# A convolution and two feed-forward layers on one core: chunk groups across the batch border, a later load of the second block, and part of the weight clipping on GpSimd

## The chip, the cores and the metric

The kernel runs on one core of a Trainium2 chip. A core has TensorE (PE: matrix products, and PEld, its loading of weights), VectorE (DVE), ScalarE (ACT), GpSimd (POOL) and SyncE (SP, which here issues nearly all transfers). Each engine works through its own instruction stream in order and waits for the others by semaphores. The metric is the device time of one execution in microseconds (us), the median of several runs.

## What is computed

There are two batches of 4096 tokens with 192 channels, so 8192 tokens. First a causal convolution over seven tokens with softmaxed taps per head, then two layers of width 2048 with weights given in float64:

```python
# convolution: 8 heads of 24 channels, 7 taps
w = softmax(weight)                       # (8, 7)
out[b, s] = sum_k w[h, k] * x_pad[b, s + k]
# layer 1
h = x @ w_in;  g = maximum(0.01 * h, h);  x = g @ w_out
# layer 2
h = x @ w_in
P = a0 + a1*h + a2*h**2 + a3*h**3
Q = 1 + |b0|*|h| + |b1|*h**2
out = (P / (Q + 1e-6)) @ w_out
```

Results are float32. Every matrix product is made of float32r products: each operand is split into a high part and a rest (`xh`/`xl`, `wiH`/`wiL`, `gH`/`gL`), and the products of the parts are added up in PSUM.

## The kernel before

The tokens are cut into 16 blocks of 512, the width of 2048 into 16 pieces j of 128. One piece of one layer for one block is five matmuls of 128x512 into a PSUM bank (`gemm1`), the nonlinearity on ACT, DVE and POOL, and five matmuls of 128x512 into an accumulator (`gemm2_hi` three, `gemm2_lo` two). Two layers, 16 blocks and 16 pieces of ten matmuls make 5,120 matmuls of 128x512.

The order is made at build time. `Planner.run` knows for each operation a rank, its engines with a cost in us, the operations before it and the buffers that it takes from a pool (four PSUM banks, 13 `work` tiles, 10 `pair` tiles, 3 `raw` tiles). It always places the operation that can start first by these costs, and where an operation names two engines (as `l2_Q`: ACT or POOL) it also picks the engine. The constants at the head of the file (`LEAD`, `STEP`, `OFF`, ...) are parts of the ranks. What the planner puts out is written down as each engine's stream, and the chip follows that order whatever the true durations are.

What matters around the change:

- **Start.** `s_warm` keeps PE at work on constants until the first data are there. The taps go to DRAM and come back as banded matrices (`s_get`, tile `band`). Blocks 0 and 1 are convolved directly: `load_x` into `xt`, `conv` (4 small products per half), `conv_evac`, transposes (`trans`), and the split into `xh`/`xl` (`x_hi`, `x_lo`). `s_fill` puts extra products on PE while it waits.
- **Blocks 2 to 15.** Chunks of 122 tokens are convolved in groups of up to five: `load_g`, `conv_g` for each half of the heads, `evac_g`, `put_g` to DRAM. `get_y`, `turn_y`, `y_hi`, `y_lo` bring them back as a block's input. `groups` is made for each batch on its own.
- **Weights.** 28 pieces, 14 a layer (`r`, `m`, `o`), come as 64-bit words and are made into float32 on the chip. In `convert`, ACT takes the magnitude (`cv_abs`) and the low word (`cv_low`), DVE clips and shifts (`cv_clip`: two instructions, lines 396 and 397, on a PSUM bank), and DVE puts the bits together (`cv_bits`: two instructions of line 250). Then ACT writes the high part (`w_hi`, `r_hi`) and DVE or POOL the rest (`w_lo`, `r_lo`).
- **End.** Layer 1 runs ahead of layer 2 by a block and more. After the last block's layer 1, its layer 2 (`l2_...`) stands alone.

Helpers record many operations, so a line of the profile is often a helper's: L253 is every matmul, L244 every activation, L247 tensor-tensor, L250 scalar-tensor-tensor, L670 `l2_Q` on POOL.

Of the kernel before, what the change touches and what calls it, by code (L numbers as in the profile page):

```python
# [27 lines left out]
STEP = 4.016
PULL = 0.005
WINDOW = 193.974  # L30
LOOK = 58
REST = -0.364
OFF = {'xfin_add': 27.93, 'xfin_main': -41.19, 'l2_rs': -6.51, 'l2_Q': -76.54, 'l2_lo': 20.05, 'cv_clip': 21.93, 'r_lo': -1.28, 'gemm2_lo': -4.32, 'fin_trans': 100.9, 'cv_abs': -25.96, 'gemm2_hi': -3.11, 'l2_R': -14.71, 'cv_low': -5.24, 'fin_evac': -75.01, 'trans': -38.96, 'mid_swap': -4.79, 'x_hi': 22.32, 'conv': -29.75, 'l2_p3': 3.44, 'r_hi': 17.48, 'x_lo': 2.67, 'fin_rest': -19.55, 'l2_abs': 22.74, 'l2_r': 2.84, 'l1_lo': -25.06, 'l2_D': -10.01, 'cv_bits': -8.15, 'l2_hi': -1.95, 'mid_add': -112.83, 'gemm1': -4.61, 'w_lo': -48.12, 'fin_add': -69.89, 'load_g': 63.41, 'conv_g': -23.42, 'evac_g': -35.87, 'put_g': 12.36, 'get_y': -27.55, 'turn_y': 19.29, 'y_hi': -15.46, 'y_lo': -20.59}
TAIL = 5.502
# [139 lines left out]
def conv_leaky_rational_kernel(  # L174
# [610 lines left out]
    on(DVE(0.4), -83, 0, s_seed, r=["qc"], w=[("xh", 1, 0, 0)])  # L785
    on(PE(0.6 * WARM + 2.2), -74, 0, s_warm, r=["ident", "qc", ("xh", 1, 0, 0)], w=[("acc", 0, 1)])
# [239 lines left out]
```

## Time and profile before

| | before |
|---|---|
| median of 3 runs | 1245.04 us (1243.78 to 1246.08) |
| the profiled execution's own time | 1244.22 us |
| its span, first to last instruction | 1242.4 us |
| busy share of PE, ACT, DVE, POOL | 98%, 92%, 90%, 85% |
| mean granted clock of TensorE | 0.996 |

The span is what the trace covers; 1.8 us of the execution's own time lie outside it. The profiled execution is 0.8 us below the median of the runs. Shares are of the span, and an average over stages of different kinds.

### The profile page before, as it was taken

To read this page: it belongs to the slowest core of one execution; us is meant where nothing else is said; L and a number is where in the kernel's file an instruction comes from. 1 tells how busy PE (TensorE), PEld (TensorE's weight loads), DVE (VectorE), ACT (ScalarE), POOL (GpSimd) and SP (SyncE) were. 2 spreads that over 40 slices of the span, in tenths; PEclk is the share of its full clock that TensorE was granted. 3 is DMA by queue.
4 is the path that set the end of the run, shared out by engine and by line. 5 is a ranking of instruction groups with operands and counts; after the bars stand their busy time and mean duration, and the time that the engine had idled before them with its cause. 6 is when DMAs were issued, how large, how long until landed. Compare 5 with 4: busy or idle time off the path is not lost.

```text
span 1242.4 us, 17891 instructions
## 1 busy us (share of the span) xinstructions
PE 1217.3 (98%) x5437; PEld 997.6 (80%) x5437; DVE 1112.0 (90%) x1671; ACT 1138.5 (92%) x1996; POOL 1059.2 (85%) x1000
## 2 busy tenths in 40 slices
PE   8999999999999999999999999999999999999976
PEld 7787788888888888888888888888888888888744
DVE  7999989898998989898988999898998989889898
ACT  6889999899999999999999999999999999999996
POOL 2787988989889898898888989899898888988886
PEclk9999999999999999999999999999999999999998
DMA  7752002020110201111010111010210002000000
GB/s 210 200 164 71 1 3 52 2 42 1 38 18 1 56 1 44 18 30 33 7 45 12 29 33 29 20 23 5 50 26 1 13 1 41 1 1 14 1 13 13
DMA packets 137414, 42.34 MB, mean 34 GB/s; under 512 B 113571, under 2 KB 134758, under 8 KB 137318
## 3 DMA queue, kind: packets, MB, share of 16 engines
q1 hardware_dynamic: 135702, 41.00, 14.3%
q8 instruction: 42, 0.69, 0.2%
q14 instruction: 54, 0.44, 0.1%
q10 hardware_dynamic: 1616, 0.21, 0.1%
HBM read 27.28 MB, written 11.80 MB: 31 GB/s over the span
## 4 chain that ended last, share of the span: by engine, by line
PE 81%; ACT 7%; DVE 7%; issue 2%; DMA 1%; POOL 1%; SPq 0%; POOLq 0%; DVEq 0%; ACTq 0%
PE bank L253 41%; PE acc L253 39%; ACT work L244 4%; DVE work L250 2%; ACT raw L244 1%; DMA raw<-in_moe_w_in_dram 1%; DVE bank L250 1%; DVE pair L247 1%; ACT bank L244 1%; DVE bank L396 1%; DVE bank L397 1%; DVE pair L250 1%; DVE work L247 0%; DVE raw L250 0%; POOL pair L247 0%
## 5 line engine op out<-in xcount | busy, mean ns | idle before, releaser
L253 PE MATMUL acc<-pair,wo 128*128 128x512 f32 x2560 | 657.4, 391 | 6.2 <-POOL pair L247 2.7
L253 PEld LDWEIGHTS acc<-pair,wo 128*128 128x128 f32 x2560 | 478.5, 188 | 110.6 <-POOL pair L247 6.9
L244 ACT ACTIVATE work<-work 128x512 f32<-128x512 f32 x532 | 331.4, 630 | 17.6 <-DVE work L250 11.0
L247 POOL TENSOR_TENSOR work<-work,pair 128x512 f32<-128x512 f32 x184 | 239.5, 1302 | 43.6 <-DVE pair L250 34.6
L253 PE MATMUL bank<-xh,wiH 128*128 128x512 f32 x512 | 203.5, 397 | 9.2 <-DVE raw L250 4.2
L253 PE MATMUL bank<-xh,wiL 128*128 128x512 f32 x512 | 200.2, 391 | 0.0
L253 PE MATMUL bank<-xl,wiH 128*128 128x512 f32 x512 | 200.0, 391 | 0.0
L253 PE MATMUL bank<-xl,wiR 128*128 128x512 f32 x512 | 200.0, 391 | 0.0
L253 PE MATMUL bank<-xh,wiR 128*128 128x512 f32 x512 | 199.9, 390 | 0.0
L250 DVE SCALAR_TENSOR_TENSOR work<-work,b_sb,bank 128x512 f32<-128x512 f32 x182 | 135.1, 742 | 46.5 <-ACT work L244 45.3
L247 POOL TENSOR_TENSOR pair<-work,work 128x512 fp32r<-128x512 f32 x122 | 158.0, 1297 | 20.4 <-DVE work L250 14.8
L250 DVE SCALAR_TENSOR_TENSOR work<-bank,a_sb,work 128x512 f32<-128x512 f32 x184 | 136.9, 744 | 9.6 <-POOL work L247 7.6
L244 ACT ACTIVATE work<-bank,a_sb 128x512 f32<-128x512 f32 x176 | 135.3, 769 | 6.1 <-PE bank L253 6.0
L250 DVE SCALAR_TENSOR_TENSOR pair<-bank,a_sb,work 128x512 fp32r<-128x512 f32 x168 | 125.2, 745 | 13.1 <-ACT work L244 7.8
L250 DVE SCALAR_TENSOR_TENSOR bank<-work,a_sb,bank 128x512 f32<-128x512 f32 x176 | 132.1, 752 | 4.1
L244 ACT ACTIVATE raw<-raw 128x512 f32<-128x512 f32 x202 | 126.8, 630 | 6.2 <-DVE raw L250 3.6
L253 PEld LDWEIGHTS bank<-xh,wiH 128*128 128x128 f32 x512 | 96.4, 188 | 38.1 <-DVE raw L250 6.6
L247 POOL TENSOR_TENSOR pair<-work,pair 128x512 fp32r<-128x512 f32 x92 | 120.3, 1308 | 7.0 <-PE acc L253 1.8
L244 ACT ACTIVATE work<-bank,b_sb 128x512 f32<-128x512 f32 x182 | 124.0, 681 | 0.0
L247 DVE TENSOR_TENSOR work<-work,bank 128x512 f32<-128x512 f32 x176 | 119.3, 678 | 1.3 <-ACT raw L244 1.3
L253 PEld LDWEIGHTS bank<-xl,wiH 128*128 128x128 f32 x512 | 96.5, 189 | 20.7 <-DVE xl L247 0.3
L253 PEld LDWEIGHTS bank<-xl,wiR 128*128 128x128 f32 x512 | 96.4, 188 | 20.6 <-DVE xl L247 0.3
(104 smaller groups left out, 1954.5 us busy)
## 6 DMA issues: line engine op xcount, KB each, us to landing
work<-y_dram SPq DMA_DIRECT2D x108, 64.0 KB
raw<-in_moe_w_out_dram SPq DMA_DIRECT2D x16, 384.0 KB
...
```

Of the source, the lines that this page charges most:

```text
L244: nc.scalar.activation(out=out_, in_=in_, func=func, **k)
L247: (eng or nc.vector).tensor_tensor(out=out_, in0=in0, in1=in1, op=op)
L250: nc.vector.scalar_tensor_tensor(out=out_, in0=in0, scalar=s, in1=in1, op0=op0, op1=op1)
L253: nc.tensor.matmul(out=out_, lhsT=w, rhs=r, start=start, stop=stop)
L396: nc.vector.tensor_scalar(out=a, in0=a, scalar1=F64_TINY, scalar2=F64_HUGE, op0=ALU.max, op1=ALU.min)
L397: nc.vector.tensor_scalar(out=ai, in0=ai, scalar1=3, scalar2=0x3FFFFFF8, op0=ALU.logical_shift_left, op1=ALU.bitwise_and)
```

## The change

Four things are done, and the ranks are set anew with them.

1. `chunks` runs through both batches, and `groups` cuts it in fives. There were 13 groups (for one batch 5, 5, 4, 4, 4, 4 chunks, for the other six of 5 and one of 4); now there are 12 of 5. The number of chunks (60) stays.
2. `load_x` of block 1 waits for both halves of `band`; `load_g` may start at rank 30 and not 8.
3. `cv_clip` is parted. The clip is an operation of its own that works in place on a `work` tile in SBUF and may go to DVE or POOL; `cv_shift` reads it and writes the PSUM bank `cb`, which `cv_bits` then uses. So a bank is held from the shift on, and no longer from `cv_abs` on.
4. `s_warm` is 13 products of 128x256, and the 19 products on a seeded tile (`s_seed`, `SHAPES`) are gone. `SP`'s cost in the planner takes 300 and not 350 KB per us.

In the new order 14 of the 28 clips are on POOL. `l2_Q` is on POOL 196 times and not 178, `l1_hi` 110 and not 93; `y_lo` is there 20 times and not 25, `w_lo` 15 and not 18, `r_lo` 3 and not 6.

```diff
-LEAD = 66.057
-GAP = 6.373
-PREP = 56.276
+LEAD = 57.54
+GAP = 12.887
+PREP = 19.279
...
-OFF = {'xfin_add': 27.93, 'xfin_main': -41.19, 'l2_rs': -6.51, ...
+OFF = {'xfin_add': 41.11, 'xfin_main': -97.37, 'l2_rs': -47.59, ...
...
-        return [("SP", max(0.6 * count, nbytes / 350e3))]
+        return [("SP", max(0.6 * count, nbytes / 300e3))]
...
-    groups = []
+    chunks = []
     for bi in range(B):
-        t0 = max(blocks[DIRECT][3] - bi * S, 0) if bi == 0 else 0
-        count = -(-(S - t0) // CG)
-        starts = [min(t0 + c * CG, S - CG) for c in range(count)]
-        ng = -(-count // NTC)
-        at = 0
-        for g in range(ng):
-            k = min(NTC, -(-(count - at) // (ng - g)))
-            groups.append((bi, starts[at:at + k], t0 + at * CG))
-            at += k
+        t0 = blocks[DIRECT][3] if bi == 0 else 0
+        while t0 < S:
+            s0 = min(t0, S - CG)
+            chunks.append((bi, s0, t0 - s0))
+            t0 = s0 + CG
+    groups = [chunks[c:c + NTC] for c in range(0, len(chunks), NTC)]
...
     def s_warm(eng):
         for n in range(WARM):
             mm(acc[0][1][:, 0:WIDE], ident, qc[:, 0:WIDE], True, True)
-        t = xh[1][0][0]
-        for cols, count, step in SHAPES:
-            for n in range(count):
-                k = n * step % 4
-                mm(acc[0][1][:, 0:cols], t[:, k * P:(k + 1) * P], t[:, 0:cols], True, True)
...
     def cv_clip(eng, l, kind, q, n):
         a = buf[("cq", l, kind, q)][:, 0:n]
-        ai = a.bitcast(I32)
-        nc.vector.tensor_scalar(out=a, in0=a, scalar1=F64_TINY, scalar2=F64_HUGE, op0=ALU.max, op1=ALU.min)
-        nc.vector.tensor_scalar(out=ai, in0=ai, scalar1=3, scalar2=0x3FFFFFF8,
+        (nc.gpsimd if eng == "POOL" else nc.vector).tensor_scalar(out=a, in0=a, scalar1=F64_TINY, scalar2=F64_HUGE,
+                                                                  op0=ALU.max, op1=ALU.min)
+
+    def cv_shift(eng, l, kind, q, n):
+        nc.vector.tensor_scalar(out=buf[("cb", l, kind, q)].bitcast(I32)[:, 0:n],
+                                in0=buf[("cq", l, kind, q)].bitcast(I32)[:, 0:n], scalar1=3, scalar2=0x3FFFFFF8,
                                 op0=ALU.logical_shift_left, op1=ALU.bitwise_and)
...
-        on(ACT(t_act(w, True)), c, 0, cv_abs, *a, w, r=[raw] + spare, w=[cq], take=("spare" if early else "bank", cq))
+        on(ACT(t_act(w, True)), c, 0, cv_abs, *a, w, r=[raw], w=[cq], take=("work", cq))
...
-        on(DVE(2 * t_dve(w, 1)), c, 0.2, cv_clip, *a, w, r=[cq] + spare, w=[cq])
-        on(DVE(2 * t_dve(w, 1)), c, 0.3, cv_bits, *a, w, r=[raw, cq, cv] + spare, w=[cq, cv])
+        on(POOL(t_pool1(w)) + DVE(t_dve(w)), c, 0.2, cv_clip, *a, w, r=[cq], w=[cq])
+        on(DVE(t_dve(w)), c, 0.25, cv_shift, *a, w, r=[cq], w=[cb], take=("bank", cb))
+        on(DVE(2 * t_dve(w, 1)), c, 0.3, cv_bits, *a, w, r=[raw, cb, cv], w=[cb, cv])
...
-        on(SP(P * k * D * 4, k), max(base - 50, 8), 2.0, load_g, g, w=[xk], extra=DMA_LAND)
+        on(SP(P * k * D * 4, k), max(base - 50, 30), 2.0, load_g, g, w=[xk], extra=DMA_LAND)
...
-        on(SP(P * ntc * D * 4, 3), max(base - 66, 4) if i else -81, 2.0, load_x, i, w=[("xt", p)],
+        on(SP(P * ntc * D * 4, 3), max(base - 66, 4) if i else -81, 2.0, load_x, i, r=[("band", 0), ("band", 1)] if i else [], w=[("xt", p)],
```

Three places show how the streams move. Numbers behind a name tell buffers apart. The first is PE's start: `xt_76` is block 0's x and `xt_77` block 1's, `ident,xc` are transposes, `qc,ident` extra products, and `xh_79 ... 128x512` the first matmuls of layer 1. Before:

```order
L253 MATMUL bank_102<-xt_76,band 103x5x24 x4
L253 MATMUL acc_96<-qc,ident 128x256
L253 MATMUL bank_99<-xt_77,band 103x5x24 x4
L547 MATMUL bank_101<-ident,xc 128x103 x4
L547 MATMUL bank_101<-ident,xc 128x100
L547 MATMUL bank_100<-ident,xc 128x103 x4
L547 MATMUL bank_100<-ident,xc 128x100
L253 MATMUL acc_96<-qc,ident 128x256
L253 MATMUL bank_102<-xt_77,band 103x5x24 x4
L253 MATMUL acc_96<-qc,ident 128x256
L253 MATMUL bank_101<-xh_79,wiH_68 128x512
L253 MATMUL bank_101<-xh_79,wiL_70 128x512
```

Now:

```order
L252 MATMUL bank_99<-xt_76,band 103x5x24 x4
L252 MATMUL acc_96<-qc,ident 128x256
L539 MATMUL bank_101<-ident,xc 128x103 x4
L539 MATMUL bank_101<-ident,xc 128x100
L539 MATMUL bank_100<-ident,xc 128x103 x4
L539 MATMUL bank_100<-ident,xc 128x100
L252 MATMUL acc_96<-qc,ident 128x256 x2
L252 MATMUL bank_99<-xh_79,wiH_68 128x512
L252 MATMUL bank_99<-xh_79,wiL_70 128x512
...
L252 MATMUL bank_99<-xt_77,band 103x5x24 x4
L252 MATMUL acc_96<-qc,ident 128x256 x4
```

Block 1's convolution has gone from ahead of the first matmuls of layer 1 to behind three pieces of them (the second half of it, not shown, to behind four).

The second place is the first weight pieces on DVE. `raw_126` is the piece `r`, `raw_127` the piece `m`, both needed by layer 1's first matmuls, `raw_128` a piece `o`; `xc` is the copy of block 0's convolution for the transposes. Before:

```order
L250 SCALAR_TENSOR_TENSOR work_104<-bank_99,work_104 128x512
L396 TENSOR_SCALAR bank_100<-bank_100 128x512
L397 TENSOR_SCALAR bank_100<-bank_100 128x512
L250 SCALAR_TENSOR_TENSOR bank_100<-raw_127,bank_100 128x512
L250 SCALAR_TENSOR_TENSOR work_106<-bank_100,work_106 128x512
L539 COPY xc<-bank_102 103x5x64
L247 TENSOR_TENSOR wiL_70<-work_106,wiH_68 128x512
L247 TENSOR_TENSOR wiR_72<-work_105,wiR_72 64x512
L247 TENSOR_TENSOR xl_87<-bank_101,xh_79 128x512
L247 TENSOR_TENSOR xl_89<-bank_100,xh_81 128x512
```

Now:

```order
L384 TENSOR_SCALAR work_106<-work_106 128x384
L388 TENSOR_SCALAR bank_100<-work_106 128x384
L388 TENSOR_SCALAR bank_102<-work_108 128x512
L249 SCALAR_TENSOR_TENSOR bank_100<-raw_128,bank_100 128x384
L249 SCALAR_TENSOR_TENSOR work_110<-bank_100,work_110 128x384
L531 COPY xc<-bank_99 103x5x64
L249 SCALAR_TENSOR_TENSOR bank_102<-raw_127,bank_102 128x512
L249 SCALAR_TENSOR_TENSOR work_109<-bank_102,work_109 128x512
L246 TENSOR_TENSOR wiR_72<-work_107,wiR_72 64x512
L246 TENSOR_TENSOR xl_87<-bank_101,xh_79 128x512
L246 TENSOR_TENSOR xl_89<-bank_100,xh_81 128x512
```

A piece `o` is converted ahead of `m`, the bits of `m` are put together behind the copy of `xc` and not ahead of it, and the rest of `m` (`wiL`) has left DVE.

The third place is POOL's start, behind the memsets and the identity. Before:

```order
L611 TENSOR_SCALAR pair_116<-work_109 128x512
L247 TENSOR_TENSOR pair_117<-work_109,pair_116 128x512
L247 TENSOR_TENSOR wo_74<-work_110,wo_74 128x2x64
L247 TENSOR_TENSOR wo_74<-work_110,wo_74 128x2x128
L611 TENSOR_SCALAR pair_120<-work_112 128x512
```

Now:

```order
L384 TENSOR_SCALAR work_108<-work_108 128x512
L246 TENSOR_TENSOR wo_74<-work_110,wo_74 128x2x64
L246 TENSOR_TENSOR wo_74<-work_110,wo_74 128x2x128
L246 TENSOR_TENSOR wiL_70<-work_109,wiH_68 128x512
L603 TENSOR_SCALAR pair_116<-work_114 128x512
L246 TENSOR_TENSOR pair_117<-work_114,pair_116 128x512
```

The clip of `m` (line 384) opens POOL's work on the weights, and `wiL` is written there behind the rest of the `o` piece.

## Rows read from the trace of the kernel before

**Rows 1.** Windows: each engine's busy us (count), granted clock, DMA share, GB/s.

```profile
15.00:105.00 90.00, 88.82 (x416) 71.90 (x415) 84.96 (x143) 78.78 (x155) 65.64 (x74) 1.00 0.59 169
...
300.00:400.00 100.00, 99.83 (x449) 82.55 (x448) 89.45 (x133) 91.44 (x162) 89.89 (x84) 1.00 0.09 18
...
1183.80:1235.60 51.80, 40.56 (x145) 27.78 (x145) 49.10 (x75) 46.70 (x80) 47.15 (x40) 0.93 0.05 8
```

**Rows 2.** The chain that ended last, pieces in order: start, us, what.

```profile
142.25 1.45 PE bank L253 x5
...
169.29 2.27 PE bank L253 x10
...
1191.32 2.52 PE bank L253 x5
```

**Rows 3.** Timeline of the start: start, us, instructions, idle time before.

```profile
2.50 5.70 PE L253 MATMUL acc<-qc,ident 128*128 128x256 f32 x16 [2.50 <-POOL ident masks.py:199]
...
9.67 0.62 ACT L244 ACTIVATE bank<-raw 128x512 f32<-128x512 f32 x1 [2.82 <-DMA raw<-in_moe_w_in_dram]
...
12.22 2.09 PE L253 MATMUL bank<-xt,band 109*103 109x120 f32 x16 [1.36 <-DMA b_sb<-in_moe_b_dram]
...
14.59 0.98 PE L253 MATMUL bank<-xt,band 109*103 109x120 f32 x8
...
14.95 0.49 DVE L539 COPY xc<-bank 103x320 f32<-103x320 f32 x1 [1.66 <-ACT xc L244]
...
15.47 0.69 DVE L247 TENSOR_TENSOR wiL<-work,wiH 128x512 fp32r<-128x512 f32 x1
...
16.91 1.29 DVE L247 TENSOR_TENSOR xl<-bank,xh 128x512 fp32r<-128x512 f32 x2
...
17.83 0.58 PE L253 MATMUL bank<-xh,wiH 128*128 128x512 f32 x1
...
18.25 0.39 PE L253 MATMUL bank<-xh,wiL 128*128 128x512 f32 x1
```

**Rows 4.** Timeline of PE behind the first two pieces of layer 1.

```profile
20.33 0.65 PE L547 MATMUL bank<-ident,xc 103*128 103x103 f32 x5
21.31 0.66 PE L547 MATMUL bank<-ident,xc 103*128 103x103 f32 x5 [0.33 <-DVE work L250]
21.81 1.91 PE L253 MATMUL acc<-qc,ident 128*128 128x256 f32 x8
```

**Rows 5.** Timeline of PE around a group's convolution in mid-run.

```profile
720.72 1.01 PE L253 MATMUL bank<-xt,band 128*122 128x120 f32 x8
721.50 1.40 PE L253 MATMUL acc<-pair,wo 128*128 128x512 f32 x5
```

**Rows 6.** Groups of DVE and POOL instructions, shapes apart: count, busy us, mean ns.

```profile
L396 DVE TENSOR_SCALAR bank<-bank 128x512 f32<-128x512 f32 x12 | 8.3, 694 | 4.7 <-ACT bank L244 4.7
...
L360 DVE CAST xh<-qc 128x512 fp32r<-128x512 f32 x1 | 0.4, 427 | 0.8 <-POOL qc L314 0.8
...
L247 POOL TENSOR_TENSOR wiL<-work,wiH 128x512 fp32r<-128x512 f32 x6 | 7.8, 1300 | 1.5 <-ACT wiH L244 1.5
...
L670 POOL TENSOR_SCALAR work<-work 128x512 f32<-128x512 f32 x124 | 78.0, 629 | 10.8 <-ACT work L244 5.7 <-ACT raw L244 4.8
```

**Rows 7.** Timeline of PE: first and last of six gaps.

```profile
41.24 0.39 PE L253 MATMUL bank<-xl,wiR 128*128 128x512 f32 x1
42.26 0.50 PE L253 MATMUL bank<-xh,wiH 128*128 128x512 f32 x1 [0.63 <-ACT work L244]
...
151.49 0.84 PE L253 MATMUL acc<-pair,wo 128*128 128x512 f32 x3
152.66 0.50 PE L253 MATMUL bank<-xh,wiH 128*128 128x512 f32 x1 [0.33 <-DVE raw L250]
```

**Rows 8.** Windows of PE near the end: busy us (count), granted clock, DMA.

```profile
1183.80:1190.00 6.20, 4.10 (x13) 1.00 0.37 63
1190.00:1194.00 4.00, 2.68 (x6) 0.62 0.00 0
```

More of the change, by code (lines that the diff above doesn't have):

```diff
@@ L19 @@
 SIZES = [512] * 16
-LEAD = 66.057
-GAP = 6.373
-PREP = 56.276
+LEAD = 57.54
+GAP = 12.887
+PREP = 19.279
 AHEAD = 40.0
-WARM = 8
-SHAPES = ((192, 6, 1), (384, 3, 1), (512, 3, 1), (256, 3, 1), (192, 4, 0))
+WARM = 13
 WIDE = 256
 FILL = {'conv': 1, 'trans': 1}
[L28 to L34, printed above, removed]
+STEP = 3.261
+PULL = 0.001
+WINDOW = 263.49
+LOOK = 37
+REST = -11.085
+OFF = {'xfin_add': 41.11, 'xfin_main': -97.37, 'l2_rs': -47.59, 'l2_Q': -93.38, 'l2_lo': 51.0, 'cv_clip': -11.79, 'r_lo': 2.32, 'gemm2_lo': -30.33, 'fin_trans': 68.44, 'cv_abs': -4.86, 'gemm2_hi': -0.55, 'l2_R': -32.59, 'cv_low': 22.32, 'fin_evac': -91.57, 'trans': -9.63, 'mid_swap': -25.77, 'x_hi': 29.97, 'conv': 13.94, 'l2_p3': -78.4, 'r_hi': 71.93, 'x_lo': -44.47, 'fin_rest': -13.48, 'l2_abs': 83.53, 'l2_r': 0.27, 'l1_lo': -13.37, 'l2_D': -17.47, 'cv_bits': 6.2, 'l2_hi': -47.88, 'mid_add': -119.21, 'gemm1': 0.17, 'w_lo': -97.03, 'fin_add': -107.14, 'load_g': 7.11, 'conv_g': -14.37, 'evac_g': 9.81, 'put_g': 32.4, 'get_y': -47.4, 'turn_y': 75.05, 'y_hi': -48.55, 'y_lo': -79.87, 'cv_shift': -26.83}
+TAIL = 4.782
 FIN = 3.219
-CV1, CV2, CV3 = -20.785, 58.237, 26.634
+CV1, CV2, CV3 = -22.59, 144.621, 37.61
 EVERY, INPLACE = 2, (1,)
@@ L468, in load_g @@
     def load_g(eng, g):
-        bi, starts, _ = groups[g]
         t = xt[g % 2]
-        for c, s0 in enumerate(starts):
+        for c, (bi, s0, _) in enumerate(groups[g]):
             if s0 == 0:
@@ L477, in zero_g @@
     def zero_g(eng, g):
-        nc.vector.memset(xt[g % 2][0:K - 1, 0, :], 0.0)
+        for c, (bi, s0, _) in enumerate(groups[g]):
+            if s0 == 0:
+                nc.vector.memset(xt[g % 2][0:K - 1, c, :], 0.0)
     def conv_g(eng, g, m):
-        k = len(groups[g][1])
+        k = len(groups[g])
         pv = buf[("gps", g, m)][0:CG, 0:k * HC].rearrange("p (t c) -> p t c", t=k)
@@ L487, in evac_g @@
     def evac_g(eng, g, m):
-        k = len(groups[g][1])
+        k = len(groups[g])
         pv = buf[("gps", g, m)][0:CG, 0:k * HC].rearrange("p (t c) -> p t c", t=k)
@@ L492, in put_g @@
     def put_g(eng, g):
-        bi, starts, t0 = groups[g]
-        for c, s0 in enumerate(starts):
-            rows = s0 + CG - (t0 + c * CG)
+        for c, (bi, s0, done) in enumerate(groups[g]):
+            rows = CG - done
             r0 = B * S - bi * S - s0 - CG
@@ L784, in conv_leaky_rational_kernel @@
     on(SP(0, 2), -60, 0, s_small, r=["tdram"], w=["ab"], extra=DMA_LAND)
[L785 to L786 removed]
+    on(PE(0.6 * WARM), -74, 0, s_warm, r=["ident", "qc"], w=[("acc", 0, 1)])
     on(ACT(0.2), -40, 0, s_abs, r=["ab"], w=["ab"])
@@ L818, in group @@
     def group(g):
-        bi, starts, _ = groups[g]
-        k, p = len(starts), g % 2
-        first = next(i for i in range(NB) if blocks[i][3] + blocks[i][2] > bi * S + groups[g][2])
+        k, p = len(groups[g]), g % 2
+        first = next(i for i in range(NB) if blocks[i][3] + blocks[i][2] > spans[g][0])
         base = t1[first * NJ] - AHEAD
         xk = ("xt", p)
-        if starts[0] == 0:
+        if any(s0 == 0 for _, s0, _ in groups[g]):
             on(DVE(0.25), base - 50, 2.0, zero_g, g, w=[xk])
-        on(SP(P * k * D * 4, k), max(base - 50, 8), 2.0, load_g, g, w=[xk], extra=DMA_LAND)
+        on(SP(P * k * D * 4, k), max(base - 50, 30), 2.0, load_g, g, w=[xk], extra=DMA_LAND)
         for m in range(2):
@@ L836, in fetch @@
         base = t1[i * NJ] - AHEAD
-        yk = [("y", g) for g, (bi, starts, t0) in enumerate(groups)
-              if bi * S + t0 < tok0 + n and bi * S + starts[-1] + CG > tok0]
+        yk = [("y", g) for g, (a, z) in enumerate(spans) if a < tok0 + n and z > tok0]
         for m in range(2):
@@ L851, in prep @@
         if i >= DIRECT:
-            while made[0] < len(groups) and groups[made[0]][0] * S + groups[made[0]][2] < blocks[i][3] + blocks[i][2]:
+            while made[0] < len(groups) and spans[made[0]][0] < blocks[i][3] + blocks[i][2]:
                 group(made[0])
```

9 lines of the change are left out of this document (3 added, 6 removed).

## The prediction

> **What bounds the kernel now.** I read the windows of all engines first, then the chain, then timelines where PE pauses. In mid-run PE is busy for 99.83 of 100 us, while DVE, ACT and POOL have 8 to 11 us left in each 100 [rows 1]. In the chain, ten matmuls of 128x512 take 2.27 us, 0.227 each [rows 2]. The 5,120 of them need 5120 x 0.227 = 1162 us of the span of 1242.4. So the middle can get shorter only by what else PE does there, and the other 80 us lie in the start, in the groups' convolutions, in pauses, and in the end. The start: PE's first layer-1 matmul runs at 17.83 us, and its second at 18.25 and not 0.227 later [rows 3]. Pauses: from 40 to 155 us I find six places where two matmuls of this size stand over 0.4 us apart; less the 0.227 they give 3.4 us. The first gives 1.02 - 0.23 = 0.79, the last 152.66 - 151.94 - 0.23 = 0.49 (the three matmuls ahead of it start at 151.49 and 0.227 apart) [rows 7]. This is the stage of the weights: from 15 to 105 us DVE is busy for 84.96 of 90 us, ACT for 78.78, POOL for only 65.64 [rows 1]. The end: from the first product of layer 2 of the last block on POOL to its last, 51.8 us, DVE is busy for 49.10, POOL for 47.15, ACT for 46.70, PE for 40.56 [rows 1]. There all three are near full and PE waits.
>
> **Groups of five.** One half-group's convolution holds PE from 720.72 to 721.50, 0.78 us [rows 5], and groups of four, looked at one by one, take 0.77 to 0.83 as well: it goes by the count of products, not by columns. Two fewer are 2 x 0.78 = 1.56 us less in a stretch where PE never rests: **-1.6 us**. The two evacuations that go with them were off the path. The groups are ready over 60 us of PE work ahead of use in both orders, so that a chunk more in some groups waits for nothing.
>
> **The first matmul.** Before, the piece m lands and ACT begins on it at 9.67; its bits are done when the copy of xc starts at 14.95; then come wiL, wiR and two xl of 0.69 and less, to 16.91 + 1.29 = 18.20 [rows 3]. Now a piece o stands ahead of m on ACT and DVE, and both wait for its transfer, which is queued behind m's. The band's transfer has one issue ahead of it where it had three, and some 80 KB less; I take it 0.3 us earlier (between 0, when nothing but bytes counts, and 0.9, the issue time saved). Then the copy of xc ends near 14.95 + 0.49 - 0.3 = 15.1. The bits of m are now behind it: two DVE instructions of 0.69 each, to 16.5; wiR to 17.2, two xl to 18.5. ACT's wiH (0.63) ends near 17.2, and wiL now runs on POOL, 1.30 us a tile [rows 6], to 18.5 at the earliest. With 0.2 for the hand-over the second matmul runs near 18.8 and not at 18.25: +0.6 us. It could be -0.3 (band 0.9 earlier, all else in time) or +1.5 (piece o lands 1 us later than I take).
>
> **What else stands at the start.** Block 1's two convolutions ran while PE waited for xl, at 14.59 and again behind the transposes; 14.59 to 15.41 is 0.82 us each [rows 3]. Now they stand among layer 1's matmuls: 2 x 0.82 = +1.6. Against it go waits that three pieces of layer 1 in a row now cover: the transposes of block 1 came at 20.33 and 21.31 though five of them take 0.5 (0.5 lost) [rows 4], and some 0.5 more in restarts up to 33 us: -1.0. The four extra products stay (eight passes). Start in all 0.6 + 1.6 - 1.0 = **+1.2 us**, between -0.7 (nothing late, and all of the 3.0 us lost behind 17.83 covered but the 1.6) and +3. The load of block 1's x is issued behind the band and five transfers more, and is needed behind three pieces of layer 1, near 18.8 + 3 x 1.13 = 22; I put that at nothing, hidden by these pieces, and at one for one if it lands later.
>
> **Clips on POOL.** In the weight stage DVE loses 14 clips (ten of 384 columns, four of 512: 10 x 0.56 + 4 x 0.69 = 8.3 us) and gains seven rests (w_lo, r_lo) and loses one, some 5.6 us at 0.69 a tile [rows 3] and 1.1 for the two parts of an o piece: -2.7 us of 85. POOL takes 14 clips, as bounded by its tensor-scalar row of 0.629 [rows 6] at most 8.8 us, and loses about 7.7: level, with 24 us of idle time for cover. The 14 clips left on DVE now run from SBUF to SBUF. No row has that operation; the bounds are 0.694, the same on a PSUM bank, and 0.427, the cast of 128x512 from SBUF to SBUF [rows 6]. I take the cast, which is nearest in its operands, so another -3 us of DVE. The Trainium skill ("VectorE: DVE Perf Modes", The perf-mode tier table) says that a 32-bit tensor-scalar runs at twice the rate when no operand is in PSUM; both rows agree with it, and by 0.694 instead I would take a third of the pauses below away and not half, 0.6 us more in the sum. A bank is also held for three DVE instructions and no longer for two engines' work. So I take half of the six pauses away: **-1.7 us**, between -3.4 (all) and +3.4 (as many again, since ACT's 78.78 us stay as they are and some pauses end on ACT [rows 7]).
>
> Where a clip waits on POOL for ACT's magnitude, and so for a transfer, the next w_lo and layer 1's gH and gL stand behind it, and gemm2_lo waits for these. POOL's 24 idle us of 90 are the cover; if they were gone, each clip would cost PE its 0.5 to 0.63 us.
>
> **The end.** In the last block POOL has 11 passes of l2_Q and ACT 5, before 7 and 9: POOL's 47.15 us become about 49.7 (4 x 0.629), ACT's fall to 44. DVE's 49.10 stay. Layer 2 starts one piece earlier against layer 1's end, PE's 1.13 us that ACT gives back. I take **+0.2 us** (POOL's idle 4.65 us shrink to 2), between -1.5 (ACT's relief reaches DVE's waits) and +2.5 (all of it shows).
>
> **Sum.** -1.6 + 1.2 - 1.7 + 0.2 = -1.9 us. From the profiled execution's 1244.2 that is 1242.3; the median of the runs is 0.8 above that execution, so I predict **1243.1 us** against 1245.04.
>
> **The rivals.** (1) *The weight stage runs free.* All six pauses go (-3.4) and ACT's relief shortens the end (-1.5): -1.6 + 1.2 - 3.4 - 1.5 = -5.3, 1239.7 us. For it: POOL was the idle engine; against: ACT is not relieved there. (2) *TensorE's clock falls at the start.* PE now ends its warm-up earlier: 26 passes, at 5.70 us for the first 16 [rows 3], so near 10 us, and has nothing until the band is there near 12, where the old one paused for 1.36 us. Near the end, after PE was busy for 4.10 of 6.20 us, the granted clock was 0.62 on average over the next 4 us [rows 8], so it lay at the lower level of 1.2 GHz for most of that. Five matmuls took 2.52 us then and 1.45 at 2.4 GHz [rows 2]. Were the first three pieces run so, 3 x 1.07 = 3.2 us: 1246.3. Against it: one pause in a busy stretch is not a stretch of half work. The Trainium skill ("TensorE: Matmul & The Clock Gate", Part 1) says that idleness lowers the clock; by the rule alone the pause could do it, and by the row of 1.36 us it did not. (3) *POOL becomes the bound in mid-run, and the kernel is slower.* POOL takes 31 more passes of l1_hi and l2_Q outside the last block's, 0.63 us each: 17 + 18 less the 4 there. Every l2_w and l2_lo stands behind them, and gemm2_lo waits for that. If half of them reach PE, 15 x 0.63 = 9.4 us, 1252.5; from seven on (-1.9 + 4.4 = +2.5, 1247.5) it is slower. Against it: in mid-run POOL has 10 us idle in 100 [rows 1], the passes add about 2, and ACT's share falls. (4) The clips move, but the stage was held by transfers: the pauses stay, -0.2 in all, 1244.8; I count it to the forecast's own spread.
>
> **How the numbers follow.** What measurement can tell from no change is about 0.2%, 2.5 us, so faster means under 1242.5. The forecast has 0.48, with its own range of 1240 to 1245.5; 0.13 of that is under 1242.5, 0.33 within, 0.02 over. Rival 1 has 0.27 (faster), rival 2 0.10 (0.08 within, 0.02 slower), rival 3 0.15 (slower). Faster 0.40, same 0.41, slower 0.19. The range of 1238.5 to 1248.5 leaves out 0.06 below (rival 1 with a start at its lower bound) and 0.13 above (rival 3's larger prices).
>
> **What would show it.** 24 half-groups in the trace and not 26, each near 0.78 us; the second matmul of layer 1 near 18.8; fewer than six pauses up to 155 us, and the clip from SBUF on DVE at 0.43; a granted clock of 1.00 from 6 to 1180 us; POOL under 93 busy us of 100 in mid-run; 52 us or so for the end. I am wrong if PE pauses in mid-run, if the clock falls near 13 us, or if a weight piece lands so late that PE stands.

## The result: 0.8% slower, nearly all of it lost before 140 us

The changed kernel takes 1254.36 us (median, 1253.1 to 1255.92) against 1244.84 for the kernel before: ratio 1.0077, 95% interval 1.0059 to 1.0095. Run again, it took 1254.53, ratio 1.0075 (1.0062 to 1.0089). For that run I had written: 

> The changed kernel once more, beside the three that follow: 1253 to 1256 us, ratio 1.0077 as before.

The page of the changed kernel, its span and the engines' busy time:

```profile
span 1251.3 us, 17826 instructions
...
PE 1216.6 (97%) x5412; PEld 998.0 (80%) x5412; DVE 1106.2 (88%) x1670; ACT 1121.0 (90%) x1962; POOL 1091.5 (87%) x1032
```

The windows that answer to [rows 1], and one of TensorE at 84 us (columns as there):

```profile
15.00:105.00 90.00, 83.23 (x388) 67.47 (x388) 75.26 (x123) 69.97 (x138) 71.40 (x68) 0.98 0.60 172
300.00:400.00 100.00, 100.00 (x450) 82.78 (x449) 89.26 (x133) 90.71 (x158) 92.78 (x88) 1.00 0.09 20
...
84.20:87.00 2.80, 2.80 (x8) 2.22 (x7) 1.38 (x3) 1.26 (x4) 2.80 (x4) 0.50 0.51 177
```

In the weight stage TensorE does less in the same 90 us (83.23 against 88.82), and so do DVE (75.26 against 84.96) and ACT (69.97 against 78.78). Only POOL does more (71.40 against 65.64), and it isn't full. Mid-run is as before. To see where the 8.9 us of span went, I took from each stretch 0.2266 us for each 128x512 matmul of the two layers that starts in it; what is left, other products included, is TensorE's loss (us):

| stretch | before | changed | difference |
|---|---|---|---|
| 0 to 40 us | 23.2 | 25.95 | +2.7 |
| 40 to 160 us | 7.6 | 15.8 | +8.2 |
| 160 to 1170 us | 21.8 | 20.9 | -0.9 |
| from 1170 us | 29.6 | 28.5 | -1.1 |

In the execution profiled the second time (span 1252.8 us) the four differences are +2.0, +7.5, -0.9 and +1.7: the start and the weight stage lose in both, the end goes either way.

The groups of the weight stage, shapes apart, from 0 to 120 us (busy us, mean ns, idle time before them):

```profile
L384 POOL TENSOR_SCALAR work<-work 128x384 f32<-128x384 f32 x10 | 15.9, 1591 | 1.5 <-ACT work L243 1.0
...
L384 POOL TENSOR_SCALAR work<-work 128x512 f32<-128x512 f32 x4 | 8.1, 2030 | 11.0 <-ACT work L243 10.8
L384 DVE TENSOR_SCALAR work<-work 128x512 f32<-128x512 f32 x8 | 6.2, 773 | 3.3 <-ACT work L243 3.3
L384 DVE TENSOR_SCALAR work<-work 128x384 f32<-128x384 f32 x6 | 2.9, 477 | 3.2 <-ACT work L243 3.2
```

A clip on POOL takes 1.59 us at 384 columns and 2.03 at 512: 24.0 us for the 14, where I had bounded them by 8.8. The largest of TensorE's waits, on its timeline and on POOL's:

```profile
80.10 0.39 PE L252 MATMUL bank<-xh,wiH 128*128 128x512 f32 x1
83.18 0.50 PE L252 MATMUL bank<-xh,wiL 128*128 128x512 f32 x1 [2.70 <-POOL wiL L246]
...
84.52 0.63 PE L252 MATMUL bank<-xh,wiH 128*128 128x512 f32 x1
84.95 0.63 PE L252 MATMUL bank<-xh,wiL 128*128 128x512 f32 x1
...
92.66 1.29 PE L252 MATMUL acc<-pair,wo 128*128 128x512 f32 x5
95.30 1.97 PE L252 MATMUL bank<-xt,band 128*122 128x120 f32 x16 [1.35 <-DVE pair L246]
```

```profile
73.28 2.26 POOL L384 TENSOR_SCALAR work<-work 128x512 f32<-128x512 f32 x1 [1.14 <-ACT work L243]
...
80.40 1.49 POOL L384 TENSOR_SCALAR work<-work 128x384 f32<-128x384 f32 x1
81.86 1.27 POOL L246 TENSOR_TENSOR wiL<-work,wiH 128x512 fp32r<-128x512 f32 x1
```

TensorE waits for a rest (wiL) that stands on POOL behind the clip of another piece, and this piece's own clip had taken 2.26 us. Behind the wait the matmuls stand 0.43 apart and the window from 84.2 shows the granted clock at 0.50, 1.2 GHz. A second wait of 2.92 us, for DVE, ends at 127.35 and has such a stretch behind it too: 14 matmuls at 0.43 in the two, 14 x 0.2 = 2.8 us of the 8.2. What DVE and TensorE waited for up to 160 us (us in total, times, longest):

```profile
DVE bank L388 <- POOL work L384: 11.3, 10, 1.8
```

```profile
PE bank L252 <- DVE pair L246: 5.1, 3, 2.9
PE bank L252 <- POOL wiL L246: 3.6, 2, 2.7
```

DVE now waits for POOL's clip, 11.3 us in ten waits, which it never did before.

### The profile page after: what moved, and what is told of

Same layout as the page of the kernel before. It is cut to its first block, busy times and chain, and to the rows that moved or that the text cites. A ratio compares the mean times of both kernels' runs of the same rounds, so it can differ in the third digit from the quotient of the medians.

```text
span 1251.3 us, 17826 instructions
## 1 busy us (share of the span) xinstructions
PE 1216.6 (97%) x5412; PEld 998.0 (80%) x5412; DVE 1106.2 (88%) x1670; ACT 1121.0 (90%) x1962; POOL 1091.5 (87%) x1032
## 4 chain that ended last, share of the span: by engine, by line
PE 86%; POOL 4%; DVE 3%; ACT 3%; DMA 2%; issue 1%; SPq 1%; POOLq 0%; ACTq 0%; DVEq 0%
PE bank L252 44%; PE acc L252 42%; ACT work L243 2%; POOL pair L246 1%; DVE work L249 1%; DMA raw<-in_moe_w_in_dram 1%; POOL work L384 1%; DVE bank L249 1%; POOL raw L246 0%; POOL work L246 0%; DVE pair L249 0%; DMA work<-work 0%; DVE raw L249 0%; DMA xt<-in_x_dram 0%; DVE pair L246 0%
## 5 line engine op out<-in xcount | busy, mean ns | idle before, releaser
L252 PE MATMUL acc<-pair,wo 128*128 128x512 f32 x2560 | 648.3, 391 | 5.3 <-POOL pair L246 4.3
L243 ACT ACTIVATE work<-work 128x512 f32<-128x512 f32 x519 | 321.3, 628 | 17.7 <-DVE work L249 11.3
L246 POOL TENSOR_TENSOR work<-work,pair 128x512 f32<-128x512 f32 x179 | 232.0, 1296 | 26.1 <-DVE pair L249 17.2
L249 DVE SCALAR_TENSOR_TENSOR work<-work,b_sb,bank 128x512 f32<-128x512 f32 x175 | 129.8, 742 | 46.2 <-ACT work L243 45.6
L243 ACT ACTIVATE work<-bank,a_sb 128x512 f32<-128x512 f32 x169 | 130.2, 770 | 19.7 <-PE bank L252 18.8
L249 DVE SCALAR_TENSOR_TENSOR pair<-bank,a_sb,work 128x512 fp32r<-128x512 f32 x177 | 131.7, 745 | 14.0 <-ACT work L243 9.1
L249 DVE SCALAR_TENSOR_TENSOR bank<-work,a_sb,bank 128x512 f32<-128x512 f32 x169 | 127.0, 751 | 3.2
L243 ACT ACTIVATE work<-bank,b_sb 128x512 f32<-128x512 f32 x175 | 119.0, 680 | 0.0
L252 PEld LDWEIGHTS bank<-xh,wiL 128*128 128x128 f32 x512 | 96.8, 189 | 22.9 <-POOL wiL L246 4.3
L246 DVE TENSOR_TENSOR work<-work,bank 128x512 f32<-128x512 f32 x169 | 114.8, 679 | 0.0
```

The costliest lines, as they stand in the source:

```text
L243: nc.scalar.activation(out=out_, in_=in_, func=func, **k)
L246: (eng or nc.vector).tensor_tensor(out=out_, in0=in0, in1=in1, op=op)
L249: nc.vector.scalar_tensor_tensor(out=out_, in0=in0, scalar=s, in1=in1, op0=op0, op1=op1)
L252: nc.tensor.matmul(out=out_, lhsT=w, rhs=r, start=start, stop=stop)
```

## The experiments

The theory that I tested: the loss is the price of the clip on POOL. The rival: it is the new order of the weight stage and the start, whatever a clip costs.

**Cheap clips in the same order.** The one edit, on POOL alone:

```diff
-    tensor_scalar(out=a, in0=a, scalar1=F64_TINY, scalar2=F64_HUGE, op0=ALU.max, op1=ALU.min)
+    tensor_scalar(out=a, in0=a, scalar1=1.0, scalar2=0.0, op0=ALU.mult, op1=ALU.add)
```

> The changed kernel in its own order, but POOL's 14 clips are a multiplication by 1 and an addition of 0 on the same tiles, the form of l2_Q (so these 14 weight pieces are not clipped). Theory (the price of max and min on POOL): the instruction takes 0.50 us at 384 columns and 0.63 at 512 in place of 1.59 and 2.03, POOL loses 24.0 - 7.5 = 16 busy us, the pauses of TensorE at 80 and at 127 us go and with them the two stretches at half clock behind them, 9 to 11 us in all: 1243 to 1246 us. Rival (the new order of the weight stage and the start): the price changes nothing on the path, pauses of 2.5 us or more stay between 75 and 135 us, 1251 to 1255 us.

1244.43 us, ratio to before 1.0004 (0.9991 to 1.0017): some 10 us less than the changed kernel. Its groups of POOL:

```profile
L385 POOL TENSOR_SCALAR work<-work 128x384 f32<-128x384 f32 x10 | 6.3, 630 | 3.4 <-ACT work L243 3.4
L385 POOL TENSOR_SCALAR work<-work 128x512 f32<-128x512 f32 x4 | 3.3, 818 | 9.4 <-ACT work L243 9.4
```

and its waits of TensorE up to 160 us:

```profile
PE bank L252 <- DVE pair L246: 2.5, 2, 1.8
...
PE bank L252 <- POOL wiL L246: 0.9, 1, 0.9
```

TensorE's loss from 40 to 160 us is 6.0 us in place of 15.8, the granted clock is 1.00 in every stretch from 17 to 1170 us, and the wait at 80 us is gone; of the one of 2.92 us 1.80 stay, ending at 118.83. The theory holds, since nothing but this instruction differs.

**The clips on DVE instead.** First in the same order (the instruction is issued to DVE at the same place), then with a new order in which the planner may choose DVE alone, then with the planner's price for POOL corrected:

```diff
-        on(POOL(t_pool1(w)) + DVE(t_dve(w)), c, 0.2, cv_clip, ...)
+        on(DVE(t_dve(w)), c, 0.2, cv_clip, ...)                        # second
+        on(POOL(0.02 + w * 0.0041) + DVE(t_dve(w)), c, 0.2, cv_clip, ...)   # third
```

> The changed kernel in its own order, but the 14 clips of POOL are issued to DVE at the same places of the sequence. Theory (the price on POOL): DVE pays 14 x 0.36 to 0.43 = 5 to 6 us more in the weight stage and POOL 24 us less; the pauses at 80 and 127 us go: 1243 to 1247 us, somewhat above the form with multiply and add, since DVE is the fuller engine. Rival (the order): 1251 to 1255 us. A second rival (DVE from SBUF is held up by POOL's subtractions, a clip then takes 1.1 to 1.3 us in place of 0.36): with 28 clips on DVE instead of 14 this comes twice as often, DVE loses 6 us more and the time stays above 1249.

> The changed kernel with DVE as the only engine that the planner may give a clip to, so the whole order is worked out anew. Theory (the price on POOL): all of the loss ahead of 140 us goes, what is left is the start and the groups of five: 1240 to 1245 us. Rival (the new order and the start): 1249 us or more. A new order differs all over, so some 2 us either way belong to it alone.

> The changed kernel with the planner's price of a clip on POOL put at 0.02 + 0.0041 us a column (1.59 at 384 columns, 2.12 at 512), as the changed kernel's trace has it, in place of 0.161 + 1/1200 a column. Theory (the loss is a wrong price): the planner gives POOL fewer clips or puts them where POOL is idle: 1240 to 1246 us. Rival (the order and the start): 1249 us or more.

1249.77 us (ratio 1.0040, 1.0027 to 1.0053), 1245.74 (1.0007, 0.9994 to 1.0020) and 1243.69 (0.9992, 0.9979 to 1.0004; seven clips stay on POOL). The third is as the theory expects, the second 0.7 us above its range. The first lies above its 1243 to 1247, where the second rival put it: 28 clips on DVE take 0.35 to 1.52 us, 17.8 in sum. That this alone makes the 4 us to the second form isn't shown: there the 28 take 0.31 to 1.49 us, 16.5 in sum, so the places in the order count too. What lengthens a clip is in the changed kernel's own trace, DVE and POOL at 25 us:

```profile
25.08 1.29 POOL L246 TENSOR_TENSOR pair<-work,pair 128x512 fp32r<-128x512 f32 x1
25.35 1.30 DVE L384 TENSOR_SCALAR work<-work 128x512 f32<-128x512 f32 x1 [0.67 <-ACT work L243]
```

DVE's clip alone takes 0.43 (6.27 to 6.70 us, nothing on POOL). Here it begins while POOL is in a subtraction, and ends 0.28 behind POOL's end (26.37). Three of the clips of the changed kernel stretch so, to 1.07 to 1.30 us, and where DVE began first, POOL's subtraction took 1.52 instead of 1.30 (from 40.61). The other two end 0.22 and 0.28 behind POOL.

**A bank between DVE and POOL.** All clips on DVE as in the second form, but the clip writes the PSUM bank and the shift is done in it:

```diff
-    tensor_scalar(out=a, in0=a, scalar1=F64_TINY, scalar2=F64_HUGE, op0=ALU.max, op1=ALU.min)
+    tensor_scalar(out=b, in0=a, scalar1=F64_TINY, scalar2=F64_HUGE, op0=ALU.max, op1=ALU.min)   # b: bank "cb"
```

> The changed kernel with all 28 clips on DVE, reading the work tile and writing a PSUM bank (the shift is then done within the bank), the order worked out anew; to be held against the run with all clips on DVE within SBUF (1245.7 us, clips of 0.31 to 1.49 us). Theory (DVE's clip within SBUF is held up by POOL's subtractions, with a bank in it it isn't): every clip takes 0.56 at 384 and 0.69 at 512 columns with no long ones, DVE's sum of clips is 16 x 0.56 + 12 x 0.69 = 17.2 us, and the time is 1243 to 1246. Rival (the long clips come of something else on DVE): clips of over 1 us stay.

Instructions of this line with the shortest, median and longest in ns, in SBUF alone and then with the bank:

```profile
L384 DVE TENSOR_SCALAR work<-work x28: 311/426/1494, 6.3 to 105.4; 128x384 f32<-128x384 f32 x16, 128x512 f32<-128x512 f32 x12
```

```profile
L384 DVE TENSOR_SCALAR bank<-work x28: 528/561/696, 6.1 to 103.1; 128x384 f32<-128x384 f32 x16, 128x512 f32<-128x512 f32 x12
```

No clip is long any more, and the time is 1242.68, ratio 0.9985 (0.9976 to 0.9994), the fastest version of the study. That the bank ends the stretching is shown; how much of the 3 us to the form in SBUF comes of it isn't, since the order was worked out anew. DVE's clips didn't get cheaper in sum: 16.9 us with the bank, 16.5 without.

**Which operation is dear on POOL.** The 14 clips of the changed kernel in five other forms:

> The changed kernel in its own order; POOL's 14 clips are done in other forms, two instructions of each: at 384 columns max alone, min alone, multiply then max, max then multiply, multiply alone; at 512 columns max alone and multiply alone (so the clip is done in part or not at all on these pieces). Theory A (a max or a min is dear on POOL by itself): each max or min costs about 0.55 us at 384 columns over the cheap form, so that one of them gives 1.0 to 1.1, two 1.59, and multiply alone 0.4 to 0.5. Theory B (one of the two is dear, or the pair of two compares leaves a fast form): max alone and multiply alone are both near 0.5, or only one of max and min is dear, or any form with one max already takes 1.5. At 512 columns by A max alone 1.3, by B 0.63 or 2.0.

A single run, 1251.84 us. Seven of the 14 on POOL's timeline, L393 with two operations, L395 with one; by their places the forms are max at 512 columns (12.00), max (29.06), min (50.13), multiply then max (67.48), multiply alone at 512 columns (71.85), max then multiply (78.02), multiply alone (108.30):

```profile
12.00 1.50 POOL L395 TENSOR_SCALAR work<-work 128x512 f32<-128x512 f32 x1 [9.67 <-ACT work L243]
...
29.06 1.17 POOL L395 TENSOR_SCALAR work<-work 128x384 f32<-128x384 f32 x1 [1.44 <-ACT work L243]
...
50.13 1.50 POOL L395 TENSOR_SCALAR work<-work 128x384 f32<-128x384 f32 x1
67.48 1.50 POOL L393 TENSOR_SCALAR work<-work 128x384 f32<-128x384 f32 x1 [0.33 <-ACT work L243]
71.85 1.50 POOL L395 TENSOR_SCALAR work<-work 128x512 f32<-128x512 f32 x1 [0.49 <-ACT work L243]
78.02 1.50 POOL L393 TENSOR_SCALAR work<-work 128x384 f32<-128x384 f32 x1
...
108.30 1.30 POOL L395 TENSOR_SCALAR work<-work 128x384 f32<-128x384 f32 x1 [0.29 <-ACT work L243]
```

Both theories fall. A single max takes 1.17 us, a min 1.50 (1.22 the other time), two operations 1.50 and more with a multiplication among them as well, and even a multiplication alone takes 1.30, and at 512 columns 1.50 like the max there. A multiplication followed by an addition is the exception: 0.51 us at 384 columns and 0.62 at 512 in the run with cheap clips, where nothing lengthened it (the longest were 0.98 and 1.07). So is l2_Q, by which I priced the clip, an addition followed by a multiplication: 0.629.

**How the dear clip reaches TensorE.** First the one rest for which TensorE waits 2.70 us is put ahead of the clip before it in POOL's queue:

```diff
+    rest, clip = at[("w_lo", 0, "m", 3)], at[("cv_clip", 0, "o", 6, 2 * D)]
+    order.insert(clip, order.pop(rest))
```

> The changed kernel with one instruction moved: on POOL the rest of piece m3 (w_lo, 80.40 instead of 81.86) stands ahead of the clip of piece o6, and nothing else differs. Theory (the wait at 80 us is the clip's place and price in POOL's queue): wiL is ready 1.5 us earlier, TensorE's wait of 2.70 us becomes 1.2, and if the stretch at half clock goes with it another 1.5 us: -1.5 to -3 us, 1251.5 to 1253. Rival (the weight stage as a whole is late by then, and a wait that is taken away at one place comes back at the next): no change, 1254 to 1255, with the later pause at 124 us longer by as much.

1254.29 us, the same as the changed kernel. Its TensorE at this place:

```profile
81.61 0.50 PE L252 MATMUL bank<-xh,wiL 128*128 128x512 f32 x1 [1.17 <-POOL wiL L246]
...
85.03 0.50 PE L252 MATMUL bank<-xh,wiH 128*128 128x512 f32 x1 [1.10 <-DVE work L249]
...
94.85 3.51 PE L252 MATMUL bank<-xt,band 128*122 128x120 f32 x16 [2.72 <-DVE pair L246]
```

The wait shrank by 1.5 us as the theory has it, but a new one of 1.10 us came 3 us later, and the one ahead of the half-groups' convolutions grew from 1.35 to 2.72. The half-clock stretch went with it: behind this wait the 16 products take 3.51 us in place of 1.97. But the changed kernel's second execution, with nothing moved, differs from its first in much the same way:

```profile
81.58 0.50 PE L252 MATMUL bank<-xh,wiL 128*128 128x512 f32 x1 [1.85 <-POOL wiL L246]
...
93.72 2.29 PE L252 MATMUL bank<-xt,band 128*122 128x120 f32 x16 [2.99 <-DVE pair L246]
```

So how much of these shifts the move made isn't shown. What counts is the time, and that stayed, as the rival has it: a wait taken away at this one place gives nothing. Two more runs part the time that POOL is held from the length of the chain through it. The first puts two multiply-and-add instructions of no use behind each cheap clip (these 14 pieces unclipped, as in the run with cheap clips); the second leaves the dear clip in place but lets it read a constant and write a tile that nobody reads:

```diff
+            for _ in range(2):                                                                    # first
+                nc.gpsimd.tensor_scalar(out=dead[:, 0:n], in0=qc[:, 0:n], scalar1=1.0, scalar2=0.0, ...)
-            nc.gpsimd.tensor_scalar(out=a, in0=a, scalar1=F64_TINY, scalar2=F64_HUGE, ...)        # second
+            nc.gpsimd.tensor_scalar(out=dead[:, 0:n], in0=qc[:, 0:n], scalar1=F64_TINY, scalar2=F64_HUGE, ...)
```

> The run with POOL's clips as multiply and add (1244.4 us), and behind each of the 14 two more instructions of that form into a tile that nobody reads, 0.5 to 0.63 us each, so that POOL is as long busy as with the dear clips (16 us more), but each piece's result is as early as with the cheap ones. Occupancy (what is queued behind the clip on POOL is late: rests, gH, gL): the loss comes back, 1252 to 1255 us. Latency (DVE's shift and bits wait for the clip itself, 10 times and 11.3 us in the changed kernel): it stays away, 1244 to 1247. Half and half: near 1249.

> The changed kernel with POOL's 14 clips at their full price and place, but reading a constant and writing a tile that nobody reads (these pieces aren't clipped), so that POOL is busy for the same 24 us and DVE's shift waits for ACT alone. Occupancy: 1251 to 1254 us. Latency: 1241 to 1246 us, with no wait of DVE for POOL's clip and POOL's own waits for ACT's magnitude gone as well. Half and half: near 1249.

1250.28 us (ratio 1.0048, 1.0033 to 1.0063), between its two ranges, and 1245.92 (1.0013, 1.0003 to 1.0023), in the range for latency. POOL's 14 places took 24.5 and 24.1 us, as in the changed kernel. The windows from 15 to 130 us of the changed kernel and of the second run:

```profile
15.00:130.00 115.00, 104.54 (x476) 84.39 (x476) 95.36 (x156) 92.60 (x177) 90.06 (x86) 0.97 0.52 147
```

```profile
15.00:130.00 115.00, 109.17 (x511) 88.64 (x510) 98.54 (x162) 99.02 (x190) 95.58 (x91) 1.00 0.55 148
```

In the second run POOL is busier (95.58 us) and costs 1.5 us over the cheap clips. So it isn't the 24 us of POOL as such. The reading that fits both: a dear clip starts only when ACT has the magnitude, and then holds both what is queued behind it and the shift that waits for it. With the queue held but the result early, 5.9 of the 10 us are lost again; the other 4 I put, by subtraction, to DVE's wait for the clip itself. The two parts need not add up in this way, each run changes what the other waits for.

**The groups.** The groups of five alone, in the kernel before (chunks and groups as in the diff, all else as it was), and the run with cheap clips with every half-group's convolution issued twice (`for hh in list(range(HB)) * 2`):

> The kernel before with the groups of five across batches and nothing else of the change; the order is worked out anew by the old table. The prediction's term: two half-groups fewer, 24 instead of 26, each 0.78 us of TensorE in a stretch in which it never rests: -1.6 us, 1242.7 against 1244.3, ratio 0.9987. Rival (a group of five is evacuated and fetched later, or the new order moves the weight stage): no gain or a loss, ratio 1.000 or more.

> The run with POOL's clips as multiply and add (1244.4 us, 24 half-groups), and every half-group's convolution issued twice. If a half-group's 0.78 us stands wholly on the path, as the sum of the prediction has it: 24 x 0.78 = +18.7 us, 1263 us. If TensorE has slack behind it (waits that shrink by as much): well under +18.7, say +5 to +14.

The doubled one takes 1262.92 us, 18.5 over the run with cheap clips, against 18.7 expected: a half-group's 0.78 us stands on the path in full, or nearly. The groups alone take 1244.71, ratio 1.0009 (0.9999 to 1.0019): no gain. From 160 to 1170 us the half-groups cost 16.2 us for 20 and not 17.7 for 22, as forecast, but two pauses that were not there give back 1.26 and 0.93. The first, DVE and POOL:

```profile
561.66 2.52 POOL L247 TENSOR_TENSOR xl<-work,xh 128x512 fp32r<-128x512 f32 x2
...
563.12 1.60 DVE L247 TENSOR_TENSOR xl<-work,xh 128x512 fp32r<-128x512 f32 x1
564.65 0.74 DVE L250 SCALAR_TENSOR_TENSOR work<-bank,a_sb,work 128x512 f32<-128x512 f32 x1
...
565.44 0.50 PE L253 MATMUL bank<-xh,wiH 128*128 128x512 f32 x1 [1.10 <-DVE work L250]
```

It looks like the same stretching: a DVE subtraction with both operands in SBUF, 1.60 us beside one of POOL's, and TensorE waits for the DVE instruction behind it. The other has a DVE subtraction of 1.52 us in the same place. Which of them meet depends on the order, so the gain of the groups between 160 and 1170 us is real and easily lost.

**Two versions of the bank form.** With the loads as before the change (`max(base - 50, 8)`, block 1's x free of the band), and with the rests of the weight pieces on POOL alone (`POOL(t_pool(w)) if n > 2`):

> The fastest form so far (all clips on DVE into a bank, 1242.7 us) with the loads as they were before: block 1's x not behind the band, the groups' x not later than before; the order worked out anew. Its start lost 2.3 us more than the kernel before up to 40 us. Theory (that loss comes of the order of the first pieces and of block 1's convolutions among layer 1, not of the loads): 1242 to 1244, the loss up to 40 us stays at 2 or more. Rival (the later load of block 1's x makes it): the loss up to 40 us falls by 1 or more and the time to 1240 to 1242.

> The fastest form so far (all clips on DVE into a bank, 1242.7 us) with the rests of the weight pieces (w_lo, both operands in SBUF) allowed on POOL alone from the fourth piece on; the order worked out anew. Theory (DVE's instructions without a PSUM operand wait for POOL's, 0.69 to 1.17 us in place of 0.37): DVE loses some 10 us of such rests, POOL has idle time for its 1.25 us each, and the pauses of TensorE between 100 and 120 us shrink: 1240 to 1242.5. Rival (POOL is the later engine there, as in the changed kernel): pauses behind wiL or wo of 1 us and more, 1243 to 1248.

The first: 1244.25 us (1.0001, 0.9989 to 1.0012), no gain over the form that it was made from. Its profiled execution, the fastest of its runs (1242.06, up to 1247.52), loses 23.9 us up to 40 us and not 25.5, which looks like the rival. But in that execution TensorE's clock stayed at 1.00 in the first convolutions, and in the other it was 0.64 from 12 to 14 us and 0.67 from 14 to 17. What the loads are worth stays open. The second: 1242.86 (0.9988, 0.9979 to 0.9997), the same as the form it was made from; TensorE's two pauses past 100 us are 1.3 and 1.0 where they were 0.6 and 1.6.

## Why the prediction was wrong

**The step that failed** is the price of POOL's clips: "POOL takes 14 clips, as bounded by its tensor-scalar row of 0.629 [rows 6] at most 8.8 us". That row is an addition and a multiplication; I took the instruction's name for its price and put no upper bound on an operation that no row had. The 14 took 24.0 us. With the price that I assumed, the changed kernel in its own order takes 1244.43 us, within the range and 1.3 above the forecast. Against 1244.34 for the kernel before beside it that is no gain where I had forecast 1.9, so the other terms together were some 2 us too good.

**The cover** was the second error of that step: "with 24 us of idle time for cover". POOL still has 18.6 idle us of 90 in the changed kernel, and TensorE loses 8 us all the same. Idle time covers an instruction that can move into it (the run with the dead clip), not one that hangs between ACT and DVE.

**Clips left on DVE.** 0.427 was right for a clip alone (0.43), 1.6 times as fast as the 0.694 on a bank. The Trainium skill ("VectorE: DVE Perf Modes", The perf-mode tier table) has such an instruction at twice the rate without an operand in PSUM; the trace agrees in kind. In the stage the mean is 0.77 at 512 columns, above the 0.694 of the PSUM form, and the 14 take 9.1 us where that form would take 8 x 0.69 + 6 x 0.56 = 8.9, so the 3 us were not there. The rule that I left out is in the Trainium skill, "SBUF — State Buffer", section SBUF: two separate sides: VectorE, in a mode that uses two ports or with two inputs in SBUF, shares a pair of SBUF ports with GpSimd, and whoever starts first has it for the whole instruction while the other stands. The clip that ends 0.28 us behind POOL's subtraction agrees with it, and so does the bank form, which has no such clip.

**The pauses, -1.7.** With cheap clips TensorE's loss from 40 to 160 us fell by 1.6, and with the dear ones it rose by 8.2, beyond my +3.4. That 1.6 meets my 1.7 is in part luck: with the cheap clips and as many matmuls in the window (415 and 416), DVE is busy for 81.16 us from 15 to 105 us, 3.8 less than before and not the 5.7 that I had counted on.

**The start, +1.2.** Right in kind, too small: up to 40 us the changed kernel loses 2.7 us more in this execution and 2.0 in the one profiled the second time. The second matmul came at 19.70 here and at 19.06 there, not at 18.8. On this kernel's timeline of the start, and on that of the same kernel the second time:

```profile
2.40 7.31 PE L252 MATMUL acc<-qc,ident 128*128 128x256 f32 x26 [2.40 <-POOL ident masks.py:199]
...
11.90 3.27 PE L252 MATMUL bank<-xt,band 109*103 109x120 f32 x16 [2.20 <-issue]
...
14.00 0.69 DVE L388 TENSOR_SCALAR bank<-work 128x512 int32<-128x512 int32 x1 [1.61 <-POOL work L384]
...
18.37 1.28 POOL L246 TENSOR_TENSOR wiL<-work,wiH 128x512 fp32r<-128x512 f32 x1 [0.44 <-ACT wiH L243]
...
19.70 0.50 PE L252 MATMUL bank<-xh,wiL 128*128 128x512 f32 x1 [0.85 <-POOL wiL L246]
```

```profile
2.40 7.87 PE L252 MATMUL acc<-qc,ident 128*128 128x256 f32 x26 [2.40 <-POOL ident masks.py:199]
11.24 2.17 PE L252 MATMUL bank<-xt,band 109*103 109x120 f32 x16 [0.97 <-issue]
...
13.44 0.69 DVE L388 TENSOR_SCALAR bank<-work 128x512 int32<-128x512 int32 x1 [1.61 <-POOL work L384]
...
19.06 0.50 PE L252 MATMUL bank<-xh,wiL 128*128 128x512 f32 x1 [0.86 <-POOL wiL L246]
```

and TensorE's clock from 12 to 14 us in the first and in the second:

```profile
12.00:14.00 2.00, 2.00 (x12) 2.00 (x13) 0.39 (x1) 1.37 (x4) 1.91 (x1) 0.54 0.94 268
```

```profile
12.00:14.00 2.00, 1.76 (x13) 1.19 (x11) 0.56 (x1) 1.75 (x5) 1.41 (x1) 1.00 1.00 303
```

Here the warm-up ends at 9.71, TensorE rests for 2.20 us, and the convolutions run at the lower level, 3.27 us for 16 and not 2.09 [rows 3]. There the same 26 products end at 10.27, the rest is 0.97 us and the clock stays. What both share is the dear clip: DVE waits 1.61 us for POOL's clip of the first piece m (1.91 and 1.92 us), and the shift, the bits of the piece o, the copy of xc, the bits of m, wiH and wiL follow. My time for the second matmul left this clip out.

To part the clip from the clock I count from ACT's first work on the piece o, one execution each, all in the same order up to there. The second matmul comes 8.84 us later here (dear clip, low clock; ACT starts at 10.86), 8.76 there (dear clip, clock at 1.00; 10.30), and 8.83 in the run with cheap clips, whose clock was at 0.71 from 12 to 14 us (19.39; 10.56). With cheap clips and the clock at 1.00 it is 7.97 in the run with the instructions of no use behind each clip (18.31; 10.34) and 7.95 in the one with every half-group doubled (18.59; 10.64). So in these executions the dear clip or the low clock costs 0.8 to 0.9 us, and here the two together no more than one; without either, my 18.8 was 0.2 to 0.5 too late. Where the clock stayed low until 19 us (the run with the one rest moved) the two gave 9.26 (19.66; 10.40). What else is lost up to 40 us I did not follow.

**The groups, -1.6,** and the end, +0.2: 24 half-groups, -1.5 us for the part between 160 and 1170, of which +0.6 came back in small pauses. From 1170 us on it is -1.1 in one execution and +1.7 in the other, so the end's +0.2 can't be judged from them.

**The rivals.** Rival 3 gave 1252.5, nearest to the time, but by another way: it is POOL that holds, in the weight stage and not in mid-run, where POOL was busy for 92.78 of 100 us and TensorE for all of it. Rival 2, the clock, came true in small: it fell near 12 us in the profiled execution, but it was up again before layer 1 and, beside the dear clip, cost next to nothing of the 3.2; in the run with the one rest moved it stayed at 0.50 from 14 to 19 us, up to the first matmul of layer 1. And it fell twice more, behind the waits of the weight stage, which I had not thought of.

## What to carry to other kernels

Price an instruction by its operations, not by its name: where the trace has the engine and the shape but not the operation, the upper bound is the dearest form that the engine shows, here the subtraction at 1.3 us, and even that was low. Idle time of an engine covers only what can be moved into it; a step put between two other engines can cost its length wherever the stage is short of time. Where VectorE and GpSimd both worked out of SBUF, one operand in PSUM on VectorE's side made the clip slower alone and even in company, 0.53 to 0.70 us for 0.31 to 1.49, though no cheaper in sum.

## What the runs showed of the chip

- GpSimd's tensor-scalar of 128x384 took 0.51 to 0.98 us as multiply and add, 1.49 to 2.03 as max and min, and 1.17 to 1.62 with one operation alone, a multiplication too. At 512 columns: 0.62 to 1.07, 1.91 to 2.26, and 1.50 to 1.67.
- A VectorE clip within SBUF that began inside a GpSimd subtraction ended 0.2 to 0.3 us behind it, in the changed kernel three times: 1.07 to 1.30 us in place of 0.36 to 0.43. With a bank as its output it took 0.53 to 0.70 beside the same work.
- TensorE's clock fell to 0.50 behind waits of 2.70 and 2.92 us in a busy stretch, and some 3 us of matmuls stood 0.43 apart each time; behind 1.85 us at the first place (the second execution) and 1.80 at the second (the run with cheap clips) it did not fall. Behind the warm-up it fell after a rest of 2.20 us in one execution of the changed kernel and not after 0.97 us in the other.
